# Attention and an MLP on one core: a new order of the block products in the first product of tiles 7 and 8

## The chip, the cores and the metric

The kernel runs on one core of a Trainium2 chip. The metric is the device time of one execution in microseconds (us), as a median over runs. Profile times are counted from the start of the span, which goes from the first to the last instruction.

## The reference

A sliding-window attention (batch 8, 8 heads, 576 positions, head size 64, window 32 to each side) gives 4608 tokens of 512 features. An MLP follows: a matrix product with `w_in` (512 x 2048), a gelu in its tanh form, and a product with `w_out` (2048 x 512).

```python
x = attention(q, k, v)            # transposed to (4608, 512)
h = x @ w_in
c = sqrt(2 / pi)
g = 0.5 * h * (1 + tanh(c * (h + 0.044715 * h**3)))
out = g @ w_out
```

## The kernel before

**Tiles.** The tokens go through the MLP in nine tiles of 512 (t = 0 to 8). For each tile, the first product gives `gT`, the gelu of x·w_in, transposed: 16 columns of 128 features on partitions and 512 tokens along the free dimension. The second product turns `gT` into 512 x 512 outputs. The attention of later batches is put between the matmuls of the second product by plans (`PLAN`, `PLAN_0`, `PLAN_1`), and the order of instructions on each engine is the order in which the program writes them (`manual_schedule`). Every engine works through its own list in that order and waits at an instruction until the data and the buffer that it needs are ready.

**Second product.** From tile 1 on it is done by a scheme of Winograd's kind with seven block products (`WINO`, L41; `ffn_out`, L718), each of 16 matmuls of 256 columns: A11·B11, S2·T2, A12·B21, S3·T3, S1·T1, A22·T4, S4·B22. I call them product 0 to product 6. The A blocks are quarters of `gT`; S1 to S4 are sums and differences of these quarters, made by VectorE in `sums` (L672 to L680), two columns per quarter at a time: `sums(t, i)` needs the columns 2i, 2i+1, 2i+8 and 2i+9 of `gT`. The products accumulate in two PSUM banks, and a new accumulation takes its bank so:

```python
        if i % 16 == 0 and new:
            pys[n % 2] = bank((1 + n) % 2)
```

So product 0 starts in bank 1 (I call it x1) and product 1 in bank 0 (x0). After product 0, the result M1 is copied out, by ScalarE in tiles 7 and 8 (L748). After product 1, VectorE makes U2 from it (L750), and only then may product 3 add to that bank.

**First product of tiles 1 to 6.** Sixteen plain blocks, `ffn_in` (L544 to L567): four matmuls of 512 columns each, then a gelu on ScalarE (L571). `column` (L540) says which column of `gT` a block number n stands for: n // 2 + 8 * (n % 2).

**First product of tiles 7 and 8** (`in_mixed`, L618 to L647). Here no attention is left to fill ScalarE and VectorE much, and half of the first product is done by the same seven-product scheme: two units, A and B, each stand for four columns (2, 3, 10, 11 for A and 4, 5, 12, 13 for B). The other eight columns are plain blocks: 0, 1, 2 (begun at the end of the tile before), 3, 12, 13, 14 and 15. `MIX` (L62) is an order written out by hand, read from left to right:

- `12`: the plain block 12, four matmuls (L563); `g12` its gelu on ScalarE (L643).
- `A3`, `B3`: block product 3 of unit A or B, four matmuls of 256 columns (`in_product`, L602, L615).
- `s0A`: a block product copied out of PSUM, by VectorE, or by ScalarE for `s1` (L630).
- `cA00`: VectorE adds a block product in PSUM to the copy (L635); this gives a finished quarter of the unit.
- `gA00`: the gelu of a finished quarter on ScalarE (L639). Quarters 00, 01 and 11 are read from SBUF (`sa`, `sb`), quarter 10 straight from PSUM.
- `t0`, `u0`: the sums S1 and S2 (`t`) and S3 and S4 (`u`) of `sums(t, 0)` (L645).

The PSUM banks of this stage: the plain blocks 3, 12 and 14 take the bank with the tag D, 13 and 15 take x0 (L556). Unit A's products 0, 1, 3 and 5 take turns in the bank O and unit B's in x1:

```python
        if n == 0:
            phs[unit, "a"] = psO.tile([128, 512], FP32, name="pu", tag="O") if unit == "A" else bank(1)
```

Products 2, and 4 with 6 added to it, take halves of two pairs of banks. `gA10` and `gB10` read the last contents of O and x1 (product 5). In the profile, tiles in x0 and x1 are called `mm`, those in D `ph`, and unit A's `pu`.

Of the kernel before, what the change touches and what calls it, by code (L numbers as in the profile page):

```python
# [36 lines left out]
def cut(b):  # L37
# [21 lines left out]

MIX = ("3 g3 A0 s0A B0 s0B A2 B2 cA00 cB00 A1 s1A A4 B1 s1B gA00 gB00 B4 t0 u0 12 A3 s3A B3 s3B g12 cA11 cB11 13 "  # L62
       "A5 B5 gA11 gB11 g13 14 gA10 gB10 A6 B6 cA01 cB01 g14 15 gA01 gB01 t1 t2 g15 t3 u1 u2 u3").split()
UNITS = {"A": 1, "B": 2}

PLAN_1 = {12: "s0@0 s1@1 s2", 16: "m0 m1", 36: "m2", 45: "v0@1 v1 s-1@0", 52: "x0", 55: "x1", 62: "m-1",
# [12 lines left out]
def kernel(  # L79
# [538 lines left out]
    def in_mixed(t):  # L618
# [4 lines left out]
        place = {"00": (0, "b"), "01": (1, "c"), "11": (2, "c")}  # L623
        for step in MIX:
            kind, rest = step[0], step[1:]
# [444 lines left out]
```

## Time and profile before

| what | value |
|---|---|
| median of 3 runs | 300.02 us (299.46 to 300.97) |
| the profiled execution's own time | 301.19 us |
| its span | 299.5 us |
| TensorE matmul busy (PE) | 286.9 us, 96% |
| VectorE busy (DVE) | 211.5 us, 71% |
| ScalarE busy (ACT) | 195.3 us, 65% |
| granted TensorE clock | 1.00 over the span |
| first product of tile 7, from its second half of blocks 0 to 2 on | 241.85 to 255.02 |
| second product of tile 7 | 255.02 to 268.36 |
| first product of tile 8 | 268.36 to 281.54 |
| second product of tile 8 | from 281.54 |

The span is what the trace covers; 1.69 us of the execution's own time lie around it. In a timeline, a row gives the start, the duration, the engine, the line in the kernel and the operation with its output and inputs; rows of the same kind in sequence are merged, and `x4` counts them. The printed end of a matmul is modelled and overlaps the next one, so that the pace of TensorE is read from start to start. Idle time before a row stands in brackets with what ended it.

### The profile page before, as it was taken

The page shows a single profiled execution, that of the slowest core. Times are in us where ns is not written, and L with a number is a line of the kernel's source. Part 1 is how long each engine was busy: PE and PEld are TensorE (multiplying, and loading weights), DVE is VectorE, ACT ScalarE, POOL GpSimd, SP SyncE. Part 2 cuts the span into 40 slices and gives each one's busy share as a digit, 9 for nine tenths or more (in the row PEclk, how much of TensorE's full clock was granted, in tenths as well). Part 3 has the DMA queues.
Part 4 walks back from the last instruction along what each step waited for, and adds up shares of the span by engine and source line. Part 5 has one row for each costly group of instructions (what it writes and reads, how often), then busy time and mean ns, then how long its engine had stood idle before and what let it go on. Part 6 is the DMA issues. An engine that isn't in the chain of part 4 may idle for free.

```text
span 299.5 us, 7284 instructions
## 1 busy us (share of the span) xinstructions
PE 286.9 (96%) x2941; PEld 184.4 (62%) x2941; DVE 211.5 (71%) x473; ACT 195.3 (65%) x313; POOL 92.5 (31%) x143
## 2 busy tenths in 40 slices
PE   8889999999899899999999999999999999999993
PEld 3534444446674488448844885488547867787683
DVE  4753577899773986767786779666876777865762
ACT  5876657779576776579566956795669556706700
POOL 3435425302664152605080506060800050015000
PEclk9999999999999999999999999999999999999999
DMA  7999998899699969998999996999690041004013
GB/s 221 271 305 383 353 285 238 233 186 204 184 221 175 209 188 197 218 148 210 175 199 142 234 157 155 143 204 183 106 205 14 0 108 36 2 13 130 0 41 103
DMA packets 115944, 50.76 MB, mean 170 GB/s; under 512 B 97495, under 2 KB 109399, under 8 KB 115910
## 3 DMA queue, kind: packets, MB, share of 16 engines
q1 hardware_dynamic: 86756, 37.62, 60.9%
q0 software_dynamic: 28032, 11.62, 26.1%
q10 hardware_dynamic: 1122, 1.06, 1.1%
q8 instruction: 23, 0.38, 0.6%
q14 instruction: 11, 0.09, 0.1%
HBM read 36.70 MB, written 9.44 MB: 154 GB/s over the span
## 4 chain that ended last, share of the span: by engine, by line
PE 58%; DMA 21%; SPq 9%; ACT 6%; DVE 3%; issue 1%; POOL 0%; DVEq 0%
PE mm L737 27%; PE mm L563 11%; PE ph L563 10%; DMA wst<-in_moe_w_in_dram 5%; SPq L182 5%; DMA kr<-in_k_dram 4%; DMA tr<-in_q_dram 4%; DMA wst<-in_moe_w_out_dram 3%; DMA KT<-k 2%; PE ps_s L454 2%; PE pu L615 2%; PE ps_d L481 2%; ACT gT L639 2%; DMA kt<-in_k_dram 2%; DMA tr<-in_k_dram 2%; DVE s L680 2%
## 5 line engine op out<-in xcount | busy, mean ns | idle before, releaser
L563 PEld LDWEIGHTS <-w_in 128*128 128x128 f16 x512 | 49.8, 98 | 56.9 <-POOL w_in L853 0.5
L563 PE MATMUL ph<-xT,w_in 128*128 128x512 f16 x256 | 64.1, 379 | 0.4 <-POOL w_in L853 0.4
L563 PE MATMUL mm<-xT,w_in 128*128 128x512 f16 x256 | 63.7, 379 | 0.0
L699 POOL DMA_DIRECT2D out_dram<-y x55 | 32.7, 604 | 84.4 <-DVE y L766 69.1
L571 ACT ACTIVATE gT<-mm 128x512 f16<-128x512 f32 x60 | 35.6, 597 | 33.2 <-PE mm L563 32.7
L737 PEld LDWEIGHTS <-s 128*128 128x128 f16 x512 | 49.4, 98 | 7.6 <-issue 0.9
L737 PE MATMUL mm<-t,s 128*128 128x256 f16 x376 | 45.0, 273 | 0.6 <-DVE y L750 0.2
L737 PEld LDWEIGHTS <-gT 128*128 128x128 f16 x384 | 36.0, 98 | 6.9 <-issue 0.5
L571 ACT ACTIVATE gT<-ph 128x512 f16<-128x512 f32 x58 | 32.2, 599 | 10.9 <-PE ph L563 10.9
L467 ACT ACTIVATE pe<-ps_s 128x960 f16<-128x960 f32 (+1 forms) x31 | 29.5, 975 | 13.6 <-PE ps_s L454 13.5
L680 DVE TENSOR_TENSOR s<-gT 128x512 f16<-128x512 f16 x64 | 27.3, 426 | 13.3 <-ACT gT L571 12.3
L737 PE MATMUL mm<-w_out,gT 128*128 128x256 f16 x256 | 32.8, 273 | 0.0
L104 ACT ACT_TABLE_LOAD x18 | 23.1, 1283 | 2.2 <-issue 1.9
L516 ACT ACTIVATE lt<-ps_d 128x480 f32<-128x480 f32 (+2 forms) x28 | 15.6, 556 | 10.8 <-PE ps_d L481 7.7
L517 ACT ACTIVATE lt<-lt 128x480 f32<-128x480 f32 (+3 forms) x36 | 21.1, 586 | 1.1
L476 DVE TENSOR_TENSOR pe<-pe,band 128x960 f16<-128x960 f16 x28 | 18.3, 670 | 1.2 <-ACT pe L467 1.2
L194 POOL DMA_DIRECT2D V<-in_v_dram x20 | 17.9, 914 | 1.3 <-PE ps_s L454 0.7
L491 PEld LDWEIGHTS <-V 128*64 128x64 f16 x520 | 14.0, 111 | 6.9 <-DVE V L204 2.3
L737 PE MATMUL mm<-t,gT 128*128 128x256 f16 x128 | 16.3, 273 | 0.0
L454 PE MATMUL ps_s<-QT,KT 64*64 64x128 f16 (+3 forms) x576 | 13.5, 216 | 1.7 <-DMA KT<-k 1.0
L454 PEld LDWEIGHTS <-KT 64*64 64x64 f16 x576 | 10.0, 106 | 7.8 <-issue 3.6
L737 PE MATMUL mm<-w_out,s 128*128 128x256 f16 x120 | 14.4, 273 | 0.0
(147 smaller groups left out, 392.8 us busy)
## 6 DMA issues: line engine op xcount, KB each, us to landing
kr<-in_k_dram SPq DMA_DIRECT2D x31, 256.0 KB, 10.8
qr<-in_q_dram SPq DMA_DIRECT2D x6, 1024.0 KB
wst<-in_moe_w_in_dram SPq DMA_DIRECT2D x7, 512.0 KB, 8.3
V<-in_v_dram POOLq DMA_DIRECT2D x20, 128.0 KB, 8.5
wst<-in_moe_w_out_dram SPq DMA_DIRECT2D x2, 1024.0 KB
wst<-in_moe_w_out_dram SPq DMA_DIRECT2D x4, 512.0 KB
qr<-in_q_dram SPq DMA_DIRECT2D x7, 256.0 KB, 7.8
out_dram<-y POOLq DMA_DIRECT2D x6, 192.0 KB, 5.8
```

The costliest lines, as they stand in the source:

```text
L104: nc.scalar.add_instruction(mybir.InstLoadActFuncSet(name=nc.get_next_instruction_name(), act_func_set_id=which, ins=[], outs=[]))
L194: nc.gpsimd.dma_start(V[:, c, :, :], v[b, :, 128 * c:128 * c + 128, :].rearrange("h p d -> p h d"))
L454: nc.tensor.matmul(sides[h][64 * half:64 * half + 64, 4 * n * r:4 * n * r + 4 * n].rearrange("k (j p) -> k j p", j=4)[:, :, p0 - q0:p1 - q ...
L467: nc.scalar.activation(pe, ps[:, :, 0:w], AF.Exp, scale=SCALE)
L476: nc.vector.tensor_tensor(pe, pe, m.rearrange("k (o j) p -> k o j p", o=1).broadcast_to(list(pe.shape)), op=ALU.mult)
L516: nc.scalar.activation(lt[:, 0:n], d[:, 0:n], AF.Ln)
L517: nc.scalar.activation(lt[:, 0:n], lt[:, 0:n], AF.Exp, scale=-1.0)
L563: nc.tensor.matmul(ph, w_in16[:, dc, fc * 128:fc * 128 + 128], xT[:, dc, t * 512 % RING:t * 512 % RING + 512], start=(dc == 0), stop=(dc = ...
L571: nc.scalar.activation(gTs[t][:, fc, :], phs[fc], AF.Gelu_apprx_tanh)
L680: nc.vector.tensor_tensor(dst, x, y, op=op)
L699: eng.dma_start(out_v[b, j, q0 + p:q0 + p + e, cols], yo[m:m + e, cols])
L737: nc.tensor.matmul(pys["apart"][:, 0:256] if apart else py[:, blk, :], lhsT, wino[w][:, f, :], start=(new and i % (8 if one else 16) == 0) ...
```

## The change

Only the list `MIX` is changed. Its entries are the same, in another order:

```diff
-MIX = ("3 g3 A0 s0A B0 s0B A2 B2 cA00 cB00 A1 s1A A4 B1 s1B gA00 gB00 B4 t0 u0 12 A3 s3A B3 s3B g12 cA11 cB11 13 "
-       "A5 B5 gA11 gB11 g13 14 gA10 gB10 A6 B6 cA01 cB01 g14 15 gA01 gB01 t1 t2 g15 t3 u1 u2 u3").split()
+MIX = ("3 g3 A0 s0A B0 s0B 12 g12 A2 B2 cA00 cB00 A1 s1A gA00 A4 B1 s1B gB00 B4 t0 u0 13 g13 A3 s3A B3 s3B 14 g14 "
+       "cA11 A5 gA10 gA11 cB11 B5 gB11 A6 cA01 B6 cB01 15 gA01 gB01 t1 t2 g15 gB10 t3 u1 u2 u3").split()
```

The plain block 12 stands behind B0 (before: behind B4), block 13 behind B4 (before: behind B3), block 14 behind B3 (before: behind B5), and block 15 where it was, behind B6. On ScalarE, `g12` moves ahead of `s1A`, `gA00` between the copies `s1A` and `s1B`, `g13` and `g14` ahead of the quarters 11, `gA10` ahead of `gA11`, and `gB10` from before `g14` to the end, behind `g15`. On VectorE the steps stand in the same order as before. TensorE has the same 5884 rows in both kernels, ScalarE, POOL and SP have the same instructions, and the lists of POOL and SP are the same in order too.

## The prediction

> **What bounds the kernel now.** I read the page first (busy shares, then the chain that ended last), then the table of stretches around the first products of tiles 7 and 8, and then the timelines of TensorE (PE), ScalarE (ACT) and VectorE (DVE) in those stretches.
>
> ```profile
> PE 286.9 (96%) x2941; PEld 184.4 (62%) x2941; DVE 211.5 (71%) x473; ACT 195.3 (65%) x313; POOL 92.5 (31%) x143
> ...
> PE 58%; DMA 21%; SPq 9%; ACT 6%; DVE 3%; issue 1%; POOL 0%; DVEq 0%
> ```
>
> PE is busy 96% of the span, and most of the chain is PE. So a change of order that adds no work can gain only PE's idle time, and loses as much as it makes PE wait. The next table shows where PE idles (columns: stretch, its length, then PE, PEld, DVE, ACT and POOL busy with counts, granted clock, DMA share, GB/s).
>
> ```profile
> 250.53:255.02 4.49, 4.49 (x30) 2.74 (x28) 3.13 (x6) 2.88 (x7) 0.00 (x0) 1.00 0.00 0
> 255.02:259.07 4.05, 3.83 (x34) 3.04 (x33) 3.43 (x9) 3.83 (x6) 0.00 (x0) 1.00 0.01 4
> 259.07:268.36 9.29, 9.29 (x92) 8.08 (x90) 6.59 (x15) 2.30 (x3) 0.25 (x1) 1.00 0.00 0
> ```
>
> The first product of tile 7 (241.85 to 255.02) leaves PE no idle time; the first 32 matmuls of the second product, behind it, do. TensorE's timeline at this seam, then ScalarE's (columns: start, duration, what):
>
> ```profile
> 253.57 0.60 PE L615 MATMUL pu<-xT,wcB 128*128 128x256 f16 x4
> 254.05 1.02 PE L563 MATMUL mm<-xT,w_in 128*128 128x512 f16 x4
> 255.02 1.91 PE L737 MATMUL mm<-w_out,gT 128*128 128x256 f16 x16
> 257.03 2.20 PE L737 MATMUL mm<-t,s 128*128 128x256 f16 x16
> 259.07 1.04 PE L737 MATMUL mm<-w_out,gT 128*128 128x256 f16 x8
> ```
>
> ```profile
> 252.28 0.63 ACT L639 ACTIVATE gT<-sa 128x512 f16<-128x512 f32 x1 [1.61 <-DVE sa L635]
> 252.88 0.63 ACT L639 ACTIVATE gT<-sb 128x512 f16<-128x512 f32 x1
> 253.42 0.58 ACT L643 ACTIVATE gT<-mm 128x512 f16<-128x512 f32 x1
> 253.90 0.59 ACT L639 ACTIVATE gT<-pu 128x512 f16<-128x512 f32 x1
> 254.37 0.60 ACT L639 ACTIVATE gT<-mm 128x512 f16<-128x512 f32 x1
> 254.85 0.61 ACT L643 ACTIVATE gT<-ph 128x512 f16<-128x512 f32 x1
> 255.33 0.65 ACT L639 ACTIVATE gT<-sa 128x512 f16<-128x512 f32 x1
> 255.85 0.65 ACT L639 ACTIVATE gT<-sb 128x512 f16<-128x512 f32 x1
> 256.37 0.62 ACT L643 ACTIVATE gT<-mm 128x512 f16<-128x512 f32 x1
> ```
>
> The reader is to see three handovers. Plain block 15 starts at 254.05; four matmuls of 512 columns take 0.87 from start to start (248.79 to 249.66 for block 12), so PE is free at 254.92. It starts product 0 at 255.02, 0.05 after the gelu of unit B's quarter 10, gB10 (254.37, from `mm`), ends at 254.97. That quarter is held in bank x1, and product 0 accumulates in x1 (L605, L726): 0.10 of waiting. Sixteen matmuls of 256 columns take 1.75 (266.61 to 268.36), so product 0 is over at 256.77; product 1 uses x0, whose reader g15 ends at 256.99, and starts at 257.03: 0.26. Product 1 takes 2.04 in place of 1.75, waiting for the sums: 0.29. Tile 8 shows the same rows 26.5 later (281.54, 283.55, 285.58), and one more wait:
>
> ```profile
> 286.92 0.69 DVE L750 TENSOR_TENSOR y<-mm,y 128x512 f32<-128x512 f32 x1
> 287.67 2.78 PE L737 MATMUL mm<-t,s 128*128 128x256 f16 x24 [0.18 <-DVE y L750]
> ```
>
> Product 3 could start at 285.58 + 1.75 = 287.33 and starts at 287.67: 0.34. So all that a better order could win at these seams is 2 x 0.65 + 0.34 = 1.64 us.
>
> **The change part by part.** No instruction is added or dropped; SP's and POOL's lists are the same, so no DMA moves past anything, and DVE's list is the same in order. PE's blocks 12, 13 and 14 come earlier, and ScalarE's gelus change order. The last is decisive: gB10, which frees x1, was ahead of g14, gA01, gB01 and g15, and is now behind them all.
>
> I recompute tile 7 with the rows of before. Handovers: a PE group's reader starts 0.20 after the next group's start (B0 at 245.74, copy of A0 at 245.94); DVE to ACT 0.03 (252.25 to 252.28); ACT to PE 0.05. Starts follow each other on ACT by 0.48 reading PSUM and 0.52 reading SBUF (rows above), on DVE by 0.60 for the float32 steps.
>
> *Front.* Block 12, now behind B0, is at its turn at 246.17, but needs the bank of block 3, whose gelu (245.65, 0.62) ends at 246.27: start 246.32, 0.15 of new waiting. From there PE's own work gives A2 247.19, A1 248.06, block 13 249.80, A3 250.67, block 14 251.54, A5 252.41, A6 253.28. The copies s1A and s1B have until 250.67 and 251.11 to free their banks and end near 249.3 and 250.3: hidden. If that cover were gone, PE would wait for them one for one.
>
> *Middle.* On DVE, s3A starts when A3 is through, 251.11 + 0.20 = 251.31; s3B 251.91, cA11 252.52, cB11 253.12 to 253.80. B6 overwrites what cB11 reads, so it starts at 253.85 and not 253.72: 0.13. Block 15 runs 254.28 to 255.15. cA01 is at 253.92, cB01 at 254.52 to 255.20.
>
> *End.* g14 can start when block 14 is through, 252.41 + 0.20 = 252.61. Then gA10 253.09, gA11 253.57, gB11 254.09, gA01 254.64, gB01 255.23 (it waits for cB01), g15 255.75, gB10 256.23 to 256.82. Product 0 starts at 256.87 and not 255.02: **1.85 later**, with PE idle 1.72 behind block 15. Behind this matmul stands everything PE has left; its queue holds nothing else to do.
>
> What goes: product 1 now finds x0 free (g15 ends at 256.37) and its sums ready. t1, t2 and t3 start at 255.32, 256.11 and 256.90 on DVE and their S2 parts end by 257.77, before product 1 even begins (258.62). So it takes 1.75, and product 2 starts at 256.87 + 3.50 = 260.37 against 259.07: **1.30 for tile 7**. Nothing takes it up later: the third line of the table has PE busy 9.29 of 9.29 us up to tile 8. Product 0's copy (behind a 1.28 table load, as before) and the last sums (until about 259.8) end well before product 2 and U2 need them.
>
> Tile 8 loses the same 1.30 up to product 2, and wins the 0.34 before product 3, since U2 then ends at about 287.8 and product 3 is due at 288.6: **0.96**. Sum: 1.30 + 0.96 = 2.26 us.
>
> What no row shows is a ScalarE queue with eight gelus waiting on mixed engines. From below: without the waits for block 3's gelu and cB01, gB10 ends 0.2 earlier, 0.4 in all: 1.9. From above: one further gelu's time (0.60) late per tile adds 1.2: 3.5. I take 2.26, since seven of the eight starts come from ScalarE's own spacing, and keep both ends.
>
> The trace has PE held at 255.02 by a bank whose reader ended 0.05 before. The Trainium skill (Perfetto Trace Analysis, Matmuls) says that independent matmul groups should rotate through banks so that one's evacuation overlaps the next group's matmuls. By this rule the new order makes the bank wanted first the one emptied last, and no overlap is left; taken alone, without what the earlier sums win back, it would make the sum 2 x 1.85 = 3.7, where the rows give 2.26.
>
> **The time.** The profiled execution took 301.19 us with a span of 299.5; 2.26 more is 303.45 with a span of 301.8. It ran 1.17 above the median of the runs, 300.02, so on the median I forecast **302.3**.
>
> **The rivals.** *Not slower.* The place is the first matmul of product 0. If x1 were free by the time block 15 ends (255.15), product 0 would lose only 0.13 against before, product 1 would keep its gain of 0.55, and tile 8's product 3 about 0.28: 0.42 + 0.70 = 1.1 faster, 298.9. It decides if gB10 ends before about 255.1. Against it: eight gelus from 252.61 at 0.48 apart cannot end before 256.5, and 255.02 already follows this very gelu. Chance 0.08.
>
> *Costlier.* ScalarE falls a further gelu behind because a DVE result comes late: cB01 already sets gB01, so whatever delays s3A to cB01 passes straight on to gB10. Price 2 x 0.60: 303.5. For it: DVE has only 0.07 of slack there; against it: its steps are evenly 0.60 apart in the trace. Chance 0.14.
>
> *Taken up.* A wait between tile 7's seam and tile 8, released by something other than PE, absorbs the 1.30: 0.96 left, 301.0. Against it is the full 9.29. Chance 0.10.
>
> **How the numbers follow.** The forecast has 0.68, within 301.7 to 302.9. The range, 300.9 to 303.9, takes in taken up, costlier and the lower bound of 1.9; only the not-slower case and tails stay out, about 0.14. What a measurement of this kernel can tell from no change is about 0.5%, 1.5 us. Slower by more: the forecast, costlier and a small part of taken up, 0.80. Within: most of taken up, of the not-slower case (1.1 us) and the forecast's lower tail, 0.17. Faster: 0.03.
>
> **What would show it.** Right: product 0 of tile 7 starts about 1.9 later, 0.05 behind the end of a gelu from `mm`; PE idles about 1.7 in front of it; product 1 takes 1.75 (1.91 as the timeline prints it, not 2.20); the wait at L750 is gone in tile 8; block 12 starts about 0.15 behind its turn. Wrong: product 0 starts at about 255.2 (the bank is not what holds it), or gB10 ends far from 256.8 (ScalarE's order runs otherwise), or tile 8 starts later by much less than 1.3.

## The result and the profile after

The changed kernel takes 304.76 us as a median of 5 runs (304.4 to 305.42) against 300.02 us before; the ratio is 1.0162, with a 95% interval of 1.014 to 1.0184. It is 4.7 us slower. I had forecast 302.3, with a range to 303.9: the sign was right, the time lies outside the range, and the loss is twice the 2.26 of the sum. Executions more than 1.5% above the fastest of the same kernel count in the medians below, but not in the ratios.

The profiled execution took 304.76 us with a span of 303.0. First, TensorE's timeline of tile 7 (start, duration, engine, line, what; idle time before it in brackets):

```profile
243.91 0.60 PE L615 MATMUL pu<-xT,w_in 128*128 128x256 f16 x4
244.34 0.60 PE L615 MATMUL mm<-xT,w_in 128*128 128x256 f16 x4
244.93 1.02 PE L563 MATMUL ph<-xT,w_in 128*128 128x512 f16 x4
...
251.01 0.60 PE L615 MATMUL pu<-xc,w_in 128*128 128x256 f16 x4
251.44 0.60 PE L615 MATMUL mm<-xc,w_in 128*128 128x256 f16 x4
252.51 0.60 PE L615 MATMUL pu<-xT,wcA 128*128 128x256 f16 x4 [0.47 <-DVE sb L635]
253.89 0.60 PE L615 MATMUL pu<-xT,wcB 128*128 128x256 f16 x4 [0.78 <-DVE sa L635]
254.33 1.03 PE L563 MATMUL mm<-xT,w_in 128*128 128x512 f16 x4
256.91 1.91 PE L737 MATMUL mm<-w_out,gT 128*128 128x256 f16 x16 [1.55 <-ACT gT L639]
258.65 1.91 PE L737 MATMUL mm<-t,s 128*128 128x256 f16 x16
260.40 1.04 PE L737 MATMUL mm<-w_out,gT 128*128 128x256 f16 x8
```

Three waits stand in brackets in it. The last one, ahead of product 0 at 256.91, is the one forecast. The two ahead of A6 (252.51) and B6 (253.89) are not: A6 was due 0.44 behind B5, at 251.88, and starts 0.63 late; B6 was due at 252.95 and starts 0.94 late. Their releasers are odd: unit A's matmuls wait for a step on `sb`, unit B's for a step on `sa`. VectorE and ScalarE in the same stretch:

```profile
251.18 0.68 DVE L635 TENSOR_TENSOR sa<-pu,sa 128x512 f32<-128x512 f32 x1
251.78 0.68 DVE L635 TENSOR_TENSOR sb<-pu,sb 128x512 f32<-128x512 f32 x1
253.15 0.69 DVE L635 TENSOR_TENSOR sa<-pu,sa 128x512 f32<-128x512 f32 x1 [0.69 <-PE pu L615]
254.53 0.69 DVE L635 TENSOR_TENSOR sb<-pu,sb 128x512 f32<-128x512 f32 x1 [0.69 <-PE pu L615]
```

```profile
253.87 0.63 ACT L639 ACTIVATE gT<-sa 128x512 f16<-128x512 f32 x1 [0.55 <-DVE sa L635]
255.25 0.63 ACT L639 ACTIVATE gT<-sb 128x512 f16<-128x512 f32 x1 [0.75 <-DVE sb L635]
255.79 0.58 ACT L643 ACTIVATE gT<-mm 128x512 f16<-128x512 f32 x1
256.27 0.59 ACT L639 ACTIVATE gT<-mm 128x512 f16<-128x512 f32 x1
```

The four VectorE rows are cA11, cB11, cA01 and cB01; the four of ScalarE are gA01, gB01, g15 and gB10. cB11 ends at 252.46, and A6 starts 0.05 later; cA01 ends at 253.84, and B6 starts 0.05 later. So the two engines take turns: cB11, A6, cA01, B6, cB01, each waiting for the one before, and then gB01, g15 and gB10 on ScalarE; product 0 follows the end of gB10 (256.86) by 0.05.

From here on I count from the start of A0 in tile 7 (245.30 before, 243.91 in the changed kernel), since what lies ahead of it differs by 1.4 us between these two profiles without any edit there. The last group of 8 matmuls starts at +48.48 before and at +53.58 after: 5.10 later. That is the loss of tiles 7 and 8, and the interval of the ratio holds it (1.014 to 1.0184 of 300 us is 4.2 to 5.5). Each tile loses 2.72 up to product 2 (before 13.77 from its A0, after 16.49); in tile 8 the wait at L750 is gone (product 2 starts at 289.63, product 3 at 291.38, 1.75 later), which gives 0.34 back: 2 x 2.72 - 0.34 = 5.10.

### The profile page after: what moved, and what is told of

It reads as the page before. It is cut to its first block, busy times and chain, and to the rows that moved or that the text cites. A ratio compares the mean times of both kernels' runs of the same rounds, so it can differ in the third digit from the quotient of the medians.

```text
span 303.0 us, 7284 instructions
## 1 busy us (share of the span) xinstructions
PE 287.2 (95%) x2941; PEld 184.5 (61%) x2941; DVE 212.5 (70%) x473; ACT 195.7 (65%) x313; POOL 92.5 (31%) x143
## 4 chain that ended last, share of the span: by engine, by line
PE 69%; DMA 16%; SPq 6%; DVE 4%; issue 1%; POOL 1%; ACT 1%; ACTq 0%; DVEq 0%
PE mm L737 31%; PE mm L563 14%; PE ph L563 12%; DMA wst<-in_moe_w_in_dram 5%; DMA tr<-in_q_dram 4%; PE pu L615 3%; PE ps_s L454 3%; DMA wst<-in_moe_w_out_dram 2%; SPq L182 2%; PE ps_d L481 2%; DMA kr<-in_k_dram 2%; DMA tr<-in_k_dram 2%; DMA qr<-in_v_dram 2%; PE ps_o L491 2%; SPq L240 2%
## 5 line engine op out<-in xcount | busy, mean ns | idle before, releaser
L680 DVE TENSOR_TENSOR s<-s,gT 128x512 f16<-128x512 f16 x32 | 13.6, 425 | 1.1
L526 DVE TENSOR_TENSOR xT<-ps_o,lt 128x480 f16<-128x480 f32 (+5 forms) x26 | 13.4, 535 | 1.1 <-PE ps_o L491 1.1
```

The costliest lines, as they stand in the source:

```text
L680: nc.vector.tensor_tensor(dst, x, y, op=op)
```

## The experiments

The theory, which I call **pair**: the products 2 and 4 of both units lie in tiles of two banks, one half for each unit, and for these tiles the program waits by the whole tile. A matmul that writes one half waits for the last read of the other half that was issued ahead of it, and a reader of one half waits for the last matmul into the other. The built program has such waits: the first matmul of A6 waits until VectorE has counted cB11, as gB11 does, and that of B6 until it has counted cA01, as gA01 does. (`gT`, a tile in SBUF, is not treated so: in the kernel before, product 0 starts at 255.02, ahead of gA01 at 255.33, which comes earlier in the program and writes another part of `gT`.) The second cause, **x1**, is the forecast one: the bank of product 0 is emptied last. The rivals: VectorE is merely **late** and TensorE waits for its own half; or the **hardware** cannot write one bank of a pair while the other is read.

The table gathers all runs. The columns "product 0", "product 2" and "last group" are starts in us from A0 of tile 7, the last from tile 8; the ratio is to the kernel before, timed on the same chip (its median was 300.02 us beside the changed kernel, 300.49 beside the next four, 300.85 beside "before, gB10 last" and the last row, 300.43 beside the other two).

| kernel | product 0 | product 2 | last group | median, us | ratio (95% interval) |
|---|---|---|---|---|---|
| before | 9.72 | 13.77 | 48.48 | 300.02 | 1 |
| changed | 13.00 | 16.49 | 53.58 | 304.76 | 1.0162 (1.014 to 1.0184) |
| changed, B6 ahead of cA01 | 12.66 | 16.15 | 52.90 | 308.06 | 1.0261 (1.0208 to 1.0314) |
| changed, a tile for each unit | 11.69 | 15.18 | 50.96 | 303.09 | 1.0093 (1.0062 to 1.0124) |
| changed, gB10 early | 11.29 | 14.78 | 50.17 | 304.27 | 1.0116 (1.0069 to 1.0163) |
| both of these | 10.03 | 13.59 | 48.12 | 300.35 | 0.9982 (0.9956 to 1.0008) |
| before, gB10 last | 11.88 | 17.04 | 53.01 | 306.62 | 1.0175 (1.0116 to 1.0235) |
| the same, gap filled | 11.88 | 15.37 | 51.35 | 304.48 | 1.0132 (1.0085 to 1.0179) |
| the same, gap open again | 11.88 | 17.04 | 53.01 | 305.93 | 1.0167 (1.0125 to 1.0208) |
| version from the findings | 9.81 | 13.37 | 47.35 | 299.28 | 0.9959 (0.9932 to 0.9986) |

The stage columns come from one profiled execution each, but are steadier than the medians: apart from the clock's part below, the waits in them repeat to some 0.02 between tiles 7 and 8 and from kernel to kernel, where executions of one kernel differ by 1 to 8 us. The verdicts on the causes rest on them.

**B6 ahead of cA01**

```diff
-... B5 gB11 A6 cA01 B6 cB01 15 ...
+... B5 gB11 A6 B6 cA01 cB01 15 ...
```

> The new order with B6 moved ahead of cA01, so that no matmul of B6 stands behind a read of its pair of banks that was issued in between. Theory 'pair': A6 and B6 wait for the last DVE read of the whole two-bank tile, the other unit's half included; so B6 no longer waits for cA01, block 15 starts 0.94 us earlier, cB01 and with it gB10 end 0.8 earlier, and the kernel takes 2 x 0.8 = 1.6 less than the changed kernel: about 303.1. A6 still waits 0.6 for cB11. Rival 'late queue': DVE is simply late and PE waits for its own halves only; then B6 starts where it did and the time stays near 304.8.

B6 starts 0.43 behind A6, without a wait, and block 15 at +9.48 and not +10.42: 0.94 earlier, as "pair" expects and "late" excludes. But product 0 gains only 0.34, not 0.8. VectorE shows why:

```profile
252.46 0.68 DVE L635 TENSOR_TENSOR sb<-pu,sb 128x512 f32<-128x512 f32 x1
254.26 0.69 DVE L635 TENSOR_TENSOR sa<-pu,sa 128x512 f32<-128x512 f32 x1 [1.12 <-PE pu L615]
254.87 0.68 DVE L635 TENSOR_TENSOR sb<-pu,sb 128x512 f32<-128x512 f32 x1
```

cA01 reads unit A's half, and A6 is through at about 253.8 (B6 starts at 253.62, and a reader follows by 0.20). It starts at 254.26, 0.20 behind the start of block 15, which is when B6 is through. The reader waits for the other unit's matmuls too: the pair holds in both directions, which my expectation had left out. The time went the other way: a median of 308.06 us, where 303.1 was expected. The profiled execution, 304.93, lies 4.4 above before, as its stages say (52.90 against 48.48); the other three took 307.31 to 309.26 at lower mean clocks (0.994 to 0.987, against 0.997). There is no trace of these, so where they lost time stays open; this profile shows no drop of the clock behind its gaps of 2.15.

**A tile for each unit**

```diff
-            if unit == "A":
-                phs[which] = psS.tile([128, 2, 512], FP32, name="pu2", tag="S1" if n == 2 else "S0")
-            phs[unit, which] = phs[which][:, "AB".index(unit), :]
+            if n == 2:
+                phs[unit] = psS.tile([128, 2, 512], FP32, name="pu2", tag="S1" if unit == "A" else "S0")
+            phs[unit, which] = phs[unit][:, "bc".index(which), :]
```

> The new order, but each unit gets one two-bank tile for its products 2 and 4, in place of one tile for both units' products 2 and one for both units' products 4. Theory 'pair': A6 waits only for cA11 and B6 only for cB11; their waits fall from 0.63 and 0.94 us to about 0.1 and 0.15, product 0 starts 1.34 earlier in each tile, and 2.7 of the loss goes: about 302.1, which is what the prediction's sum gives (302.3). What is left is the bank x1, freed last. Rival 'late queue': no change, near 304.8. Rival 'hardware': a matmul cannot write one bank of a pair while DVE reads the other, so that the waits stay as stretched matmuls: also near 304.8.

The same four banks, otherwise shared out. TensorE's timeline of tile 7:

```profile
251.26 0.60 PE L615 MATMUL pu<-xc,w_in 128*128 128x256 f16 x4
251.69 0.60 PE L615 MATMUL mm<-xc,w_in 128*128 128x256 f16 x4
252.17 0.60 PE L615 MATMUL pu<-xT,wcA 128*128 128x256 f16 x4
252.76 0.60 PE L615 MATMUL pu<-xT,wcB 128*128 128x256 f16 x4
253.20 1.03 PE L563 MATMUL mm<-xT,w_in 128*128 128x512 f16 x4
255.78 1.91 PE L737 MATMUL mm<-w_out,gT 128*128 128x256 f16 x16 [1.55 <-ACT gT L639]
```

A6 starts 0.48 behind B5 and B6 0.59 behind A6: waits of 0.04 and 0.15 in place of 0.63 and 0.94. A6 writes a bank of unit A's pair while cB11 (252.03 to 252.71) still reads unit B's. With "late" the two waits would have stayed. The coupling shows in a new place: A4 writes one bank of unit A's tile and cA00 reads the other until 247.30, and A1 and A4 together take 0.94 (246.84 to 247.78) and not 0.87. "Hardware" is not tested by this, since the two banks now lie in different pairs. Against it stand the matmuls of A6 and B6 in the changed kernel, which are held back but not stretched (0.60 as everywhere), and the waits in the program, which explain the delay without it; no run writes one bank of a pair while the other is read. The last group comes 2.62 earlier, and 2.48 of the loss stay: this is the kernel that my sum of 2.26 priced, without knowing it. The time agrees, 1.0093 or 2.8 us.

**gB10 early**

```diff
-... B5 gB11 A6 cA01 B6 cB01 15 gA01 gB01 t1 t2 g15 gB10 t3 ...
+... B5 gB11 gB10 A6 cA01 B6 cB01 15 gA01 gB01 t1 t2 g15 t3 ...
```

> The new order with gB10 moved from behind g15 to behind gB11, into idle time of ScalarE. Theory 'x1': product 0 starts when block 15 is through (about 0.87 after its start) and not 2.58 after it, which takes 1.7 us off each tile: about 301.4, with the waits of A6 and B6 unchanged at 0.63 and 0.94. If the bank were not what holds product 0, the time would stay near 304.8; if it were the only cause, 300.0 would be reached.

```profile
255.38 1.03 PE L563 MATMUL mm<-xT,w_in 128*128 128x512 f16 x4
256.25 1.91 PE L737 MATMUL mm<-w_out,gT 128*128 128x256 f16 x16
```

Product 0 starts 0.87 behind block 15, at once, and 1.71 earlier than in the changed kernel: "x1" holds to 0.01. A6 and B6 wait as before, 0.63 and 0.94. 1.69 of the loss stay in the stages. The four runs (302.57 to 305.27) give 3.5 us, more than that, with an interval from 2.1; the profiled execution is the shortest of them, and where the others were longer stays open.

**Both**

> The new order with one two-bank tile for each unit and gB10 behind gB11. Both causes gone: block 15 is through 9.98 us after A0's start (before: 9.62), product 0 starts there at once, products 1 and 2 follow without a wait, so that product 2 starts 13.5 after A0 (before: 13.77; changed kernel: 16.49), and in tile 8 product 3 at 15.7 (before: 15.86). The sum is 0.2 per tile faster than before at most: about 299.6, not to be told from 300.0. If a third cause were at work, over 301.

Product 2 starts at +13.59 and the last group at +48.12, 0.36 ahead of before; the time can't be told from before. With both causes gone the loss is gone, and no third one shows. They do not simply add: alone they leave 1.69 and 2.48, together 5.10, which is 0.93 more than the sum. Of this, 0.36 is what the new order wins once both are gone, and 0.33 is the wait at L750 in tile 8, which is back in this kernel (product 3 starts at 285.35, due at 285.02) and absent from the changed kernel and from each of the two single edits; the rest is 0.12 per tile.

**Before, with gB10 last**

```diff
-... g13 14 gA10 gB10 A6 B6 cA01 cB01 g14 15 gA01 gB01 t1 t2 g15 t3 ...
+... g13 14 gA10 A6 B6 cA01 cB01 g14 15 gA01 gB01 t1 t2 g15 gB10 t3 ...
```

> The kernel before with one entry moved: gB10 from behind gA10 to behind g15, the other part of the change alone. Theory 'x1': g14, gA01, gB01 and g15 follow each other about 0.5 earlier, gB10 ends last at about 11.8 after A0's start, product 0 starts at 11.85 (before: 9.72), products 1 and 2 then run without a wait, and product 2 starts at 15.35 (before: 13.77): 1.6 per tile, less 0.34 for product 3 in tile 8: 2.8 in all, about 302.9. A6 and B6 don't wait, since block 14 still stands between B5 and A6. With the 1.0 per tile that the changed order with gB10 early costs, the parts add up to the whole if they share no wait. Rival: if the order of the blocks were what makes the bank late, no change: 300.0.

Product 0 starts at +11.88, as expected. But the median is 306.62 us, where 302.9 was expected, and in tile 7 the two products behind the wait take 5.16 in place of 3.49; in tile 8, behind the same gap, they don't. This was not in any theory, so two kernels follow on one chip: the same again, and one with the gap filled by matmuls.

```diff
                 ffn_in(t, int(step), then=False)
+                if step == "15":
+                    spin(16, 256)
```

> The kernel before with gB10 behind g15, and 16 matmuls of 256 columns whose result nobody reads put behind block 15 in tiles 7 and 8, so that TensorE works through 1.75 of the 2.1 us that it waits there. Theory 'clock': the 2.1 us of idle time let the granted clock fall now and then (0.61 and 0.74 in the 5 us behind it in one profile), which makes the time longer than the stages add up to; filled, the clock stays at 1.00 there, product 2 starts at 15.3 after A0, and the time is 2.8 above before with little spread: about 303. Rival 'noise': the spread comes from elsewhere; then the time and its spread are those of the same kernel with the gap open, about 305.5 and 303.9 to 310.

> The kernel before with gB10 behind g15 once more, on the same chip as the one with the filled gap, as its control. Theory 'clock': again above the 303 that the stages give, with some executions at 305 and more, and mean clocks under 0.995 in these. Rival 'noise': the two kernels have the same median within 1 us.

The table of stretches with the gap open (stretch, length, PE, PEld, DVE, ACT and POOL busy, granted clock, DMA share, GB/s), first tile 7, then tile 8; and after it with the gap filled, tile 7:

```profile
254.86:257.99 3.13, 1.02 (x6) 0.38 (x4) 2.81 (x6) 3.11 (x7) 0.00 (x0) 1.00 0.00 0
257.99:263.15 5.16, 5.16 (x33) 3.99 (x33) 2.87 (x9) 1.84 (x2) 0.00 (x0) 0.67 0.02 3
284.64:287.77 3.13, 1.02 (x6) 0.38 (x4) 2.80 (x6) 3.08 (x6) 0.00 (x0) 1.00 0.00 0
287.77:291.26 3.49, 3.49 (x32) 3.13 (x32) 2.87 (x9) 0.58 (x1) 0.00 (x0) 1.00 0.00 0
```

```profile
253.74:256.87 3.13, 2.77 (x22) 1.95 (x20) 2.81 (x6) 3.11 (x7) 0.00 (x0) 1.00 0.00 0
256.87:260.36 3.49, 3.49 (x32) 3.12 (x32) 2.86 (x9) 1.84 (x2) 0.00 (x0) 1.00 0.02 5
```

Behind 2.1 us of idle time the granted clock is 0.67 over the next 5.16 us of tile 7, and 1.67 us are lost (3.49 / 5.16 is 0.68); with the gap filled by matmuls nobody reads, the clock stays at 1.00 and product 2 starts at +15.37, where 15.3 was expected. That the lost time is the clock's is shown. That the gap sets it off fits these stages, but rests on one profile with the gap filled, and the same gap in tile 8 brought no drop. In the medians the difference is 1.45 us on one chip (305.93 against 304.48), but the intervals of the two ratios overlap, so the times alone don't decide between "clock" and "noise"; and 304.48 is itself 1.2 above the 2.87 that the stages give. The mean clocks over whole executions are 0.98 to 0.993 with the gap open and 0.991 to 0.999 with it filled.

**A version from the findings**

```diff
-... s0A B0 s0B 12 g12 A2 B2 cA00 ...
+... s0A B0 s0B A2 12 g12 B2 cA00 ...
...
-                sums(t, int(rest), slice(0, 2) if kind == "t" else slice(2, 4))
+                sums(t, int(rest), slice(0, 2) if kind == "t" else slice(2, 4 if rest == "0" else 3))
...
             nc.vector.tensor_tensor(U2, py, M1, op=ALU.add)
+            if t >= NT - 2:
+                for j in range(1, 4):
+                    sums(t, j, slice(3, 4))
```

These edits stand on top of a tile for each unit and gB10 early.

> A version built from the findings: one two-bank tile for each unit, gB10 behind gB11, block 12 behind A2 in place of B0 (its bank is free there, 0.15 less per tile), and the S4 sums of columns 1 to 3 behind U2 on DVE (product 3 of tile 8 no longer waits, 0.33). Against the version with one tile for each unit and gB10 early: 0.6 less; the last group of matmuls starts 47.5 after A0 of tile 7 (before: 48.48, changed kernel: 53.58). About 299.1, 0.9 below before, hardly to be told from it by the time alone. Wrong if block 12 still waits or U2 still starts behind the sums.

Block 12 starts without a wait, product 3 of tile 8 too, and the last group at +47.35, 1.13 ahead of before (47.5 was expected). The time is 299.28 us, 0.9959 of before (0.9932 to 0.9986): the interval leaves out 1, so it is a little faster than before, by some 0.4%.

## Why the prediction was right in its sign and wrong in its size

One row of the kernel before bears on the middle step, VectorE's cA01 in tile 7:

```profile
254.20 0.69 DVE L635 TENSOR_TENSOR sa<-pu,sa 128x512 f32<-128x512 f32 x1 [1.36 <-PE pu L615]
```

- *Front.* Right. Block 12 was due at 244.78 and starts at 244.93: the 0.15 of the text.
- *Middle.* **This step failed.** It had A6 starting on time and B6 late by 0.13, since "B6 overwrites what cB11 reads". It took each half of a pair as a buffer of its own. In fact A6 waits for cB11 and B6 for cA01: 0.63 and 0.94. Before the change, the first wait lay behind block 14 (cB11 ended at 252.84, A6 started at 253.13), and no read stood between A6 and B6 at all. The change moved the block away and put cA01 between them. The code shows it, one tile with `"AB".index(unit)` as its half. The waits of A6 and B6 themselves could not be seen before, since the cover was complete, but the coupling could, in the other direction: in the row above, A6 was through when B6 started, at 253.57, so that a reader of unit A's half alone was due at 253.77. cA01 started 0.43 later, 0.20 behind the end of B6. With a tile for each unit the waits fall to 0.04 and 0.15, close to what the step had priced.
- *End.* The mechanism was right. gB10 frees x1 last, product 0 follows it by 0.05, products 1 and 2 run without a wait, and L750 no longer holds product 3. TensorE idles 1.71 behind block 15, where 1.72 was forecast. Only the start of the chain was late: cB01 came later by the failed step, and product 0 with it, at +13.00 where +11.57 was forecast. These 1.43 per tile are the whole miss of the sum: 2.26 + 2 x 1.43 = 5.12, against 5.10 in the stages.
- *The bank rule* of the Trainium skill (Perfetto Trace Analysis, Matmuls), rotate so that evacuation overlaps, speaks rightly against the change: moving the one evacuation back gives 1.71 per tile.
- *The rivals.* "Costlier" had the right carrier, a late VectorE result that passes straight on to gB10, and priced it at 0.60 per tile, with the remark that VectorE's steps are evenly 0.60 apart. In the changed kernel they are so only up to cB11 (251.78); cA01 and cB01 follow at 253.15 and 254.53. The 0.07 of slack that it names was none: in the sum, cB01 already held gB01 back by that much (255.23 and not 255.16). "Taken up" did not happen: TensorE has no wait between product 2 of tile 7 and tile 8. "Not slower" needed x1 to be free early; with gB10 early and without the pair it comes to 300.35 us, which can't be told from before, and not to 298.9.
- *The bounds.* The upper one, 3.5, was one gelu per tile. The failed step had no bound of its own: what a wait would cost if a tile and not a bank were its unit could have been worked out from the prediction's own numbers: A6 not before cB11's end, so at 253.85, B6 not before the end of cA01, which itself follows A6, so at 255.23 and not 253.85. By this estimate the sum is 2.26 + 2 x 1.38 = 5.0.

## What to carry to other kernels

When an order is rewritten by hand, list for each instruction the last access to the whole PSUM tile that stands ahead of it, not just to its part: here two users of one tile were coupled by the order of their accesses, even in different banks. A block of independent work between a read and the next write is the cover of that pair, and moving it away uncovers the wait. The buffer that the next stage takes first should be emptied first, and a wait of TensorE can cost more than its length: behind two of the six gaps of 2.1 us in these profiles the granted clock fell too.

## What the runs showed of the hardware that was not expected

Behind a TensorE gap of 2.1 us the granted clock fell, to 0.67 on average over the next 5.16 us, in both profiles of the kernel with gB10 last, in tile 7 but not behind the same gap in tile 8, and not behind the two gaps of 2.15 us in the profile with B6 ahead of cA01. Behind the gaps of 1.55 us (as the profile prints them, like the others here), in the changed kernel and with a tile for each unit, it stayed at 1.00. The Trainium skill (TensorE: Matmul & The Clock Gate, Part 1: The HAM clock gate) says that the clock is throttled after at least one idle window of about 3.4 us; here it fell behind 2.1 us with matmuls on both sides, and the measurement decides. Why the drop comes behind one such gap and not behind another stays open.
